# Linear attention and two feed-forward layers: how the keys are loaded, projected and multiplied out

## The chip, the core and the metric

The kernel runs on one core of one Trainium2 chip. Five engines matter: TensorE (PE, matrix products), VectorE (DVE), ScalarE (ACT), GpSimd (POOL) and SyncE (SP), whose queue issues nearly all transfers. The metric is the device time of one execution in microseconds (us); the median of three runs is compared.

## What is computed

Three stages follow one another. The attention is linear: keys and queries of 32 numbers are mapped to 64 features, the outer product of two projections of 8 numbers each.

```python
def phi(x):                                   # q, k, v: 4 batches, 4 heads, 1088 tokens, 32 numbers
    a = np.einsum('rd,bhsd->bhsr', S1, x)     # S1, S2: 8 x 32
    b = np.einsum('rd,bhsd->bhsr', S2, x)
    return np.einsum('bhsi,bhsj->bhsij', a, b).reshape(*x.shape[:-1], r * r)
q_p, k_p = (phi(q), phi(k))
kv = np.einsum('bhsf,bhsd->bhfd', k_p, v)
z = np.sum(k_p, axis=2)
num = np.einsum('bhsf,bhfd->bhsd', q_p, kv)
den = np.einsum('bhsf,bhf->bhs', q_p, z)[..., None] + 1e-06
x = num / den                                 # to 4352 tokens x 128
# feed-forward: 128 -> 1536 -> 128, gated
xn = x / sqrt(mean(x * x) + 1e-06) * rms_g
x = (silu(xn @ w_gate) * (xn @ w_val)) @ w_out
# soft mixture: 32 slots, 8 experts of 128 -> 1024 -> 128, combined back to the tokens
```

The weights and S1, S2 come as float64 words and are turned into float32 on the chip.

## The kernel before, in words

The 4352 tokens go through the feed-forward layer in nine tiles: eight of 512 tokens (two for each batch) and one of 256 with the last 64 tokens of every head (the "short" rows). A tile has 12 slots, one for each 128 of the 1536 hidden columns; a slot has three passes each for gate and value (high and low parts of float32) and three for the output, or one product in full float32 in tile 0. While these run, chains of small steps for the next tiles are set between them: `k_chain(b)` prepares the keys of a batch, `q_chain(T)` the queries of a tile.

Ahead of the first tile stands a part without feed-forward work, the front. Its order is written out by hand in the table `FRONT`, a string of tokens that `front()` reads one by one; each token calls one step, and all steps of one engine stay in this order. `kt:0`, `kt:1` and `kt:2` transpose the two halves of the keys and the short keys on DVE; `bm` places the two forms of S1 and S2 (`bdk`, `bd`) that the products take; `kp` projects the keys and `kg` the short keys on PE; `kx:0`, `kx:1` turn the projections of two heads each by a transpose on DVE (PSUM to SBUF); `ko:0`, `ko:1`, `ko:2` are the outer products of heads 0 and 1, of heads 2 and 3, and of the short keys; `kv` copies the values beside a column of ones on ACT; `ks:0`, `ks:1` sum features times values on PE; `kw`, `kb`, `kl` spread, transpose and place these sums. `qs`, `qp`, `qh`, `qo`, `qb` are the same steps for the queries of tile 0, `qa` multiplies them with the placed sums, `qd` divides, `qq` to `ql` normalize. `c:n` is one step of the conversion of weight piece n (five steps: ACT, DVE, ACT, DVE, POOL, and for gate and value pieces a split into high and low parts on ACT and POOL). `n:x` are x products of constants that keep PE busy.

Behind the front, a scheduler orders the work; it keeps each engine's queue in order, so that an instruction that waits holds all that stands behind it on its engine. The later batches (b = 1, 2, 3) go through `k_chain`.

Transfers: `load` puts each on SP. The order is S1 and S2 (on ACT's queue), keys, half of the queries, short keys, values, short values, then the weights by turns. The keys of a batch lie in a tile of 128 partitions; `c` is the half of it that one transposition and one product take. The product `project` has the 128 x 64 tile `bdk` as its stationary side and the 512 transposed columns of one half as its moving side; half c writes the output partitions 64 c to 64 c + 63 of one PSUM bank.

## Time and profile before

| what | us |
|---|---|
| runs of before, median (lowest, highest) | 314.44 (314.32, 315.17) |
| the profiled execution | 314.38 |
| its span, first to last instruction | 312.6 |
| PE busy | 302.9 |
| DVE busy | 234.8 |
| ACT busy | 178.2 |
| POOL busy | 64.5 |

Busy times are sums over the whole span, and the stages have different limits; what an engine's work is worth is read stage by stage. PE's products are pipelined, and their ends are modelled: a start of the next one is a better measure of what a product costs than its own length. In a row of a timeline, a bracket tells how long the engine stood idle before it and who released it.

### The profile page before, as it was taken

The page shows a single profiled execution, that of the slowest core. Times are in us where ns is not written, and L with a number is a line of the kernel's source. Part 1 is how long each engine was busy: PE and PEld are TensorE (multiplying, and loading weights), DVE is VectorE, ACT ScalarE, POOL GpSimd, SP SyncE. Part 2 cuts the span into 40 slices and gives each one's busy share as a digit, 9 for nine tenths or more (in the row PEclk, how much of TensorE's full clock was granted, in tenths as well). Part 3 has the DMA queues.
Part 4 walks back from the last instruction along what each step waited for, and adds up shares of the span by engine and source line. Part 5 has one row for each costly group of instructions (what it writes and reads, how often), then busy time and mean ns, then how long its engine had stood idle before and what let it go on. Part 6 is the DMA issues. An engine that isn't in the chain of part 4 may idle for free.

```text
span 312.6 us, 5481 instructions
## 1 busy us (share of the span) xinstructions
PE 302.9 (97%) x1933; PEld 235.9 (75%) x1933; DVE 234.8 (75%) x461; ACT 178.2 (57%) x399; POOL 64.5 (21%) x111
## 2 busy tenths in 40 slices
PE   8899989999999999999999999999999999999993
PEld 4676755778885778888867788888787778898482
DVE  4879956886797968878779878787787667666862
ACT  2568574385563376665533765654574655566562
POOL 3659899000601010020010100100020100003220
PEclk9999999999999999999999999999999999999999
DMA  5997100010033100010331000100991493000016
GB/s 154 243 383 220 33 1 0 2 25 11 0 125 95 26 4 0 11 25 0 118 100 25 6 0 12 25 0 14 332 221 23 134 305 101 0 2 1 2 46 242
DMA packets 43627, 23.97 MB, mean 77 GB/s; under 512 B 18896, under 2 KB 39632, under 8 KB 43600
## 3 DMA queue, kind: packets, MB, share of 16 engines
q1 hardware_dynamic: 43424, 23.56, 26.8%
q8 instruction: 15, 0.25, 0.4%
q10 hardware_dynamic: 176, 0.07, 0.1%
q14 instruction: 12, 0.10, 0.1%
HBM read 19.81 MB, written 2.23 MB: 71 GB/s over the span
## 4 chain that ended last, share of the span: by engine, by line
PE 82%; DMA 5%; SPq 4%; DVE 3%; ACT 3%; issue 2%; DVEq 0%
PE v L676 7%; PE g L676 7%; PE v L677 7%; PE o L676 7%; PE v L678 7%; PE g L677 7%; PE g L678 7%; PE o L678 7%; PE o L677 7%; SPq L78 4%; PE aux L563 4%; DMA ring<-in_moe_w_val_dram 2%; PE aux L420 2%; PE o L742 2%; PE aux L379 2%; DMA ring<-in_moe_w_out_dram 2%
## 5 line engine op out<-in xcount | busy, mean ns | idle before, releaser
L717 ACT ACTIVATE silu<-g 128x512 f32<-128x512 f32 (+1 forms) x103 | 60.9, 593 | 52.7 <-PE g L678 51.8
L718 DVE TENSOR_TENSOR hf<-v,silu 128x512 f32<-128x512 f32 (+1 forms) x91 | 61.3, 675 | 19.4 <-PE v L678 10.3
L727 ACT CAST hh<-hf 128x512 fp32r<-128x512 f32 x89 | 54.8, 616 | 36.6 <-DVE hf L718 36.3
L732 DVE TENSOR_TENSOR hl<-hf,hh 128x512 fp32r<-128x512 f32 x89 | 61.4, 691 | 15.2 <-ACT hh L727 14.4
L676 PE MATMUL g<-xh,wgh 128*128 128x512 f32 (+1 forms) x107 | 43.5, 407 | 0.9 <-ACT silu L717 0.9
L676 PE MATMUL v<-xh,wgh 128*128 128x512 f32 (+1 forms) x107 | 42.9, 401 | 0.0
L678 PE MATMUL g<-xl,wgh 128*128 128x512 f32 (+1 forms) x107 | 40.9, 382 | 0.0
L677 PE MATMUL v<-xh,wgl 128*128 128x512 f32 (+1 forms) x107 | 40.7, 381 | 0.0
L678 PE MATMUL v<-xl,wgh 128*128 128x512 f32 (+1 forms) x107 | 40.7, 380 | 0.0
L677 PE MATMUL g<-xh,wgl 128*128 128x512 f32 (+1 forms) x107 | 40.5, 379 | 0.0
L676 PE MATMUL o<-hh,woh 128*128 128x512 f32 (+1 forms) x94 | 37.1, 395 | 0.0
L678 PE MATMUL o<-hl,woh 128*128 128x512 f32 (+1 forms) x94 | 36.5, 389 | 0.0
L677 PE MATMUL o<-hh,wol 128*128 128x512 f32 (+1 forms) x94 | 35.9, 382 | 0.0
L611 POOL TENSOR_SCALAR rs<-ss 128x4 f32<-128x4 f32 (+1 forms) x8 | 2.4, 301 | 139.1 <-ACT sq L604 139.0
L676 PEld LDWEIGHTS g<-xh,wgh 128*128 128x128 f32 x107 | 20.2, 188 | 6.9 <-ACT silu L717 2.0
L676 PEld LDWEIGHTS v<-xh,wgh 128*128 128x128 f32 x107 | 20.1, 188 | 5.5 <-issue 1.9
L677 PEld LDWEIGHTS g<-xh,wgl 128*128 128x128 f32 x107 | 20.1, 188 | 4.7 <-issue 1.0
L677 PEld LDWEIGHTS v<-xh,wgl 128*128 128x128 f32 x107 | 20.1, 188 | 4.2 <-issue 1.1
L678 PEld LDWEIGHTS v<-xl,wgh 128*128 128x128 f32 x107 | 20.1, 188 | 4.1 <-issue 0.2
L678 PEld LDWEIGHTS g<-xl,wgh 128*128 128x128 f32 x107 | 20.1, 188 | 4.0 <-DVE work L318 0.2
L676 PEld LDWEIGHTS o<-hh,woh 128*128 128x128 f32 x94 | 17.7, 188 | 4.2 <-issue 1.4
L678 PEld LDWEIGHTS o<-hl,woh 128*128 128x128 f32 x94 | 17.7, 188 | 3.1 <-issue 0.2
(272 smaller groups left out, 504.1 us busy)
## 6 DMA issues: line engine op xcount, KB each, us to landing
ring<-in_moe_w_dram SPq DMA_DIRECT2D x12, 256.0 KB, 7.7
ring<-in_moe_w_dram SPq DMA_DIRECT2D x5, 512.0 KB, 5.0
ring<-in_k_dram SPq DMA_DIRECT2D x8, 256.0 KB, 3.4
ring<-in_v_dram SPq DMA_DIRECT2D x16, 128.0 KB, 2.9
ring<-in_moe_w_gate_dram SPq DMA_DIRECT2D x6, 256.0 KB, 6.7
ring<-in_moe_w_val_dram SPq DMA_DIRECT2D x6, 256.0 KB, 6.1
ring<-in_moe_w_out_dram SPq DMA_DIRECT2D x3, 512.0 KB, 7.2
qt<-in_q_dram SPq DMA_DIRECT2D x3, 512.0 KB, 5.3
```

Source lines behind the costliest of these rows:

```text
L78: i = (on or nc.sync).dma_start(out=out, in_=in_)
L379: pe.matmul(self.a["k"][64 * c : 64 * c + 64, :], bdk.rearrange("p h r -> p (h r)"), self.kT[c], start=True, stop=True)
L420: pe.matmul(self.a["kv", hp][64 * h2 : 64 * h2 + self.cols, 64 * hp : 64 * hp + 64], (va_all if t < 8 else vr_all)[:, v0 : v0 + self.cols] ...
L563: pe.matmul(o, pD[:, f, h, :], rhs, start=(f == 0), stop=(f == 1))
L676: first = pe.matmul(o, ah, bh, start=start, stop=False)
L677: pe.matmul(o, al, bh, start=False, stop=False)
L678: last = pe.matmul(o, ah, bl, start=False, stop=stop)
L717: mark["silu"] = act.activation(s[:, cs], g[:, cs], AF.Silu).ins
L718: mark["gate"] = mark["gate", T, f] = dve.tensor_tensor(out=hf32[T, f][:, cs], in0=v[:, cs], in1=s[:, cs], op=ALU.mult).ins
L727: act.copy(hh[T, f], hf32[T, f])
L732: dve.tensor_tensor(out=hl[T, f], in0=hf32.pop((T, f)), in1=hh[T, f].bitcast(F32), op=ALU.subtract)
L742: last = pe.matmul(ops[T][:, 0:w], w_c, h[:, cs], start=(c == 0), stop=(c == NF - 1))
```

## The change

Six things are changed together.

1. The keys of a batch are loaded by four transfers to 64 partitions each, where there were two to 128. Which token lies where is changed so that half c holds the tokens 512 c to 512 c + 511.
2. The short keys are loaded by one transfer to 128 partitions (256 bytes each), where there were four to 32 (two pieces of 128 bytes each). Its source has the four heads outermost, then 32 pairs of tokens.
3. The values are loaded by one transfer with 1 KB pieces, where there were four to 64 partitions with 512-byte pieces.
4. `project` issues eight products of 128 columns, where there were two of 512: for each head the two halves by turns. In the front the first two heads go to one bank and the last two to another, so that `kx:0` can begin after four of them. In the later batches the short keys' product stands ahead of them, and each product is held behind the one before it.
5. In the front the outer product of heads 2 and 3 is shared: one half on POOL, one on DVE, where POOL did both. The second part of the queries' outer product is POOL's instead of DVE's, for which ACT copies the second projection out of PSUM as well.
6. The table `FRONT` is written in another order: `kv:1` comes before `qh` and `kh`, and the weight steps `c:0` between the sums and their transposition move behind it.

```diff
--- before.py
+++ after.py
@@ -29,8 +29,8 @@
 
 
 FRONT = """
-n:17 b n:4 kz kt:0 bm kt:1 bm qs kt:2 kp kx:0 kx:1 ko:0:d ko:1:p qp kg kv:0 kh ko:2:d qh kv:1 n:4 km
-ks:0 qo:0 qo:1 qb c:0 ks:1 kw:0:a c:0 c:0 kb:0 kw:1:a n:2 kb:1 n:10 c:0 kl:0:a kl:1:d c:0 c:1 c:0 c:1 c:0
+n:17 b n:3 kz kt:0 bm kt:1 bm qs kp kt:2 kx:0 kx:1 ko:0:d ko:1:p:0 ko:1:d:1 qp kg kv:0 kv:1 qh kh ko:2:d qo:1:p n:4 km
+ks:0 qo:0:d qb c:0 ks:1 kw:0:a kb:0 kw:1:a n:2 kb:1 n:10 c:0 c:0 kl:0:a kl:1:d c:0 c:1 c:0 c:1 c:0 c:0
 qa:0 qa:1 n:26 qd:0 qd:1 qq:0:a qq:1:d qr:0 qq:2:a qq:3:d qr:1 c:1 kr:a qm:0 qm:1 qt:0 qx:0 n:2 qt:1 qx:1 c:1 c:1 ql c:2 c:2 c:2 c:1 c:2
 """
 
@@ -96,23 +96,23 @@
 
         t = ring()
         kt[b] = t.rearrange("p (h c m) -> p h c m", h=H, c=2)
+        src = k[b, :, 0:1024, :].rearrange("h (c u e n) d -> c e u h (n d)", c=2, e=2, n=4)
         for c in range(2):
-            src = k[b, :, 0:1024, :].rearrange("h (p c n) d -> c p h (n d)", c=2, n=4)[c]
-            load(out=kt[b][:, :, c], in_=src)
+            for e in range(2):
+                load(out=kt[b][64 * e : 64 * e + 64, :, c], in_=src[c, e])
 
     def load_kr(b):
-        kr[b] = sb.tile([P, 2, D], F32, tag="kr", name="kr")
-        for h in range(H):
-            load(out=kr[b][32 * h : 32 * h + 32], in_=k[b, h, 1024:, :].rearrange("(n x) d -> x n d", n=2))
+        kr[b] = sb.tile([P, 2 * D], F32, tag="kr", name="kr")
+        load(out=kr[b], in_=k[b, :, 1024:, :].rearrange("h (x n) d -> h x (n d)", n=2))
 
     def load_v(b):
 
         t = ring()
         vt[b] = t.rearrange("p (h n d) -> p h n d", h=H, d=D)
-        src = v[b, :, 0:1024, :].rearrange("h (e u c n) d -> c e u h (n d)", e=2, c=2, n=4)
-        for c in range(2):
-            for e in range(2):
-                load(out=t.rearrange("p (h e m) -> p e h m", h=H, e=2)[64 * c : 64 * c + 64, e], in_=src[c, e])
+        load(
+            out=t.rearrange("p (h n) -> p h n", h=H),
+            in_=v[b, :, 0:1024, :].rearrange("h (p j) d -> p h (j d)", j=8),
+        )
         load(out=vr[:, :, 0:D], in_=v[b, :, 1024:, :].rearrange("h p d -> p h d"))
 
     def load_q(b):
@@ -354,7 +354,7 @@
             self.kvz = kvz[b] = sb.tile([P, 2, H, 4, D1], F32, tag="kvz", name="kvz", bufs=2)
             self.pk = [work().rearrange("p (h t n) -> p h t n", h=2, t=8) for _ in range(2)]
             self.pk.append(sb.tile([P, H, 1, R * R], F32, tag="pkr", name="pkr"))
-            self.kT, self.a, self.x = {}, {}, {}
+            self.kT, self.a, self.x, self.last = {}, {}, {}, None
             self.cols = 64 if b == 0 else D1
 
         def zero(self):
@@ -366,25 +366,31 @@
                 dve.transpose(self.kT[c].rearrange("p (h m) -> p h m", h=H), kt[self.b][:, :, c])
             else:
                 self.kT[c] = sb.tile([P, 64], F32, tag="krT", name="krT")
-                dve.transpose(self.kT[c], kr[self.b].rearrange("p n d -> p (n d)"))
+                dve.transpose(self.kT[c].rearrange("p (x n) -> p n x", n=2), kr[self.b])
 
         def copy_v(self, hp, eng):
             hs = slice(2 * hp, 2 * hp + 2)
             src = vt[self.b][:, hs].rearrange("p h t d -> p (h t) d")
             eng(va[:, hs, :, 0:D].rearrange("p h t d -> p (h t) d"), src)
 
-        def project(self):
-            self.a["k"] = bank()
-            for c in range(2):
-                pe.matmul(self.a["k"][64 * c : 64 * c + 64, :], bdk.rearrange("p h r -> p (h r)"), self.kT[c], start=True, stop=True)
+        def project(self, banks=1):
+            for h in range(H):
+                if h == 0 or h == 2 and banks == 2:
+                    a = bank()
+                self.a["k", h // 2] = a
+                cs = slice(P * h, P * h + P)
+                for c in range(2) if banks == 2 else (1, 0):
+                    with tc.issue_after(self.last) if self.last else nullcontext():
+                        o = a[64 * c : 64 * c + 64, cs]
+                        self.last = pe.matmul(o, bdk.rearrange("p h r -> p (h r)"), self.kT[c][:, cs], start=True, stop=True).ins
 
         def project_r(self):
             self.a["r"] = bank()
-            pe.matmul(self.a["r"][0:64, 0:64], self.kT[2], bdf, start=True, stop=True)
+            self.last = pe.matmul(self.a["r"][0:64, 0:64], self.kT[2], bdf, start=True, stop=True).ins
 
         def turn(self, hps, dst):
             cs = slice(256 * hps.start, 256 * hps.stop)
-            dve.transpose(dst[:, cs], self.a["k"][:, cs])
+            dve.transpose(dst[:, cs], self.a["k", hps.start][:, cs])
             x = dst.rearrange("p (g r) -> p g r", r=2 * R)
             for hp in range(hps.start, hps.stop):
                 gs = slice(16 * hp, 16 * hp + 16)
@@ -393,7 +399,7 @@
         def halves_r(self):
             self.x[2] = proj_halves(self.a["r"], 4, 64)
 
-        def outer(self, g, on=dve):
+        def outer(self, g, on=dve, es=slice(0, 2)):
             x1, x2 = self.x[g]
             pp, n = x1.shape[0], x1.shape[1]
             if g < 2:
@@ -401,10 +407,8 @@
             else:
                 dst = self.pk[g][:pp].rearrange("p h j n -> p (h j) n")
 
-            m = 2 if on is pool else 1
-            for e in range(m):
-                es = slice(n // m * e, n // m * (e + 1))
-                outer(dst[:, es], x1[:, es], x2[:, es], on)
+            es = slice(n // 2 * es.start, n // 2 * es.stop)
+            outer(dst[:, es], x1[:, es], x2[:, es], on)
 
         def sum(self, hp, ts, banks=1):
 
@@ -479,14 +483,15 @@
                 pool.memset(kvT[32:64], 0.0)
             for hp in range(2):
                 k.copy_v(hp, pool.tensor_copy)
-        for c in range(2):
+        for c in (0, 1):
             yield POST, 1
             with tc.issue_after(mark["gate"]):
                 k.transpose(c)
-        k.transpose(2)
+                if c == 0:
+                    k.transpose(2)
         yield PE, 0
+        k.project_r()
         k.project()
-        k.project_r()
         yield POST, 1
         k.turn(slice(0, 2), row("x2"))
         k.halves_r()
@@ -542,9 +547,13 @@
         def halves(self):
             self.pq = work()[:, 0 : 256 * self.n].rearrange("p (f g n) -> p f g n", f=2, n=D)
             self.x1, self.x2 = proj_halves(self.a["q"], 4 * self.n, P)
-
-        def outer(self, f):
-            outer(self.pq[:, f], self.x1[:, :, 4 * f : 4 * f + 4], self.x2)
+            if self.T == 0:
+                x2 = sb.tile([P, P], F32, tag="asb", name="asb", bufs=3).rearrange("p (g r) -> p g r", r=R)
+                act.copy(x2, self.x2)
+                self.x2 = x2
+
+        def outer(self, f, on=dve):
+            outer(self.pq[:, f], self.x1[:, :, 4 * f : 4 * f + 4], self.x2, on)
 
         def back(self):
             pD = work()[:, 0 : 256 * self.n]
@@ -940,11 +949,11 @@
             "bm": lambda: next(placed, None),
             "kz": k.zero,
             "kt": lambda c: k.transpose(int(c)),
-            "kp": k.project,
+            "kp": lambda: k.project(2),
             "kg": k.project_r,
             "kx": lambda hp: k.turn(slice(int(hp), int(hp) + 1), turned),
             "kh": k.halves_r,
-            "ko": lambda g, e="d": k.outer(int(g), on[e]),
+            "ko": lambda g, e="d", half=None: k.outer(int(g), on[e], slice(int(half), int(half) + 1) if half else slice(0, 2)),
             "kv": lambda hp: k.copy_v(int(hp), act.copy),
             "ks": lambda hp: k.sum(int(hp), range(9), 2),
             "kw": lambda hp, e: k.spread_1(int(hp), copy[e]),
@@ -955,7 +964,7 @@
             "qs": q.shuffle,
             "qp": q.project,
             "qh": q.halves,
-            "qo": lambda f: q.outer(int(f)),
+            "qo": lambda f, e: q.outer(int(f), on[e]),
             "qb": q.back,
             "qa": lambda m: q.attend(int(m)),
             "qd": lambda m: q.divide(int(m)),
```

Two places show what this does to the queues. First DVE in the front, from the transposition of the first queries on (`x` are the queries, `silu` the turned projections, `work` the outer products, `pkr` that of the short keys, `kvz` the placed sums, `cvt` and `cvs` the first weight piece). Before:

```order
L535 STREAM_TRANSPOSE x_201<-x 128x512
L369 STREAM_TRANSPOSE krT<-kr 128x64
L387 STREAM_TRANSPOSE silu<-aux 128x256 x2
L318 TENSOR_TENSOR work<-silu 128x1024
L318 TENSOR_TENSOR pkr<-asb,v 64x256
L318 TENSOR_TENSOR work<-asb,g 128x512 x2
L551 STREAM_TRANSPOSE work<-work 128x1024
L220 TENSOR_SCALAR cvt<-cvt 128x512
L225 SCALAR_TENSOR_TENSOR cvs<-ring,cvt 128x512
L462 COPY kvz<-aux 32x4x33 x4
```

The same place after the change:

```order
L540 STREAM_TRANSPOSE x_196<-x 128x512
L369 STREAM_TRANSPOSE krT<-kr 128x2x32
L393 STREAM_TRANSPOSE silu<-aux 128x256
L393 STREAM_TRANSPOSE silu<-g 128x256
L318 TENSOR_TENSOR work<-silu 128x1024
L318 TENSOR_TENSOR work<-silu 128x512
L318 TENSOR_TENSOR pkr<-asb,aux 64x256
L318 TENSOR_TENSOR work<-asb 128x512
L560 STREAM_TRANSPOSE work<-work 128x1024
L220 TENSOR_SCALAR cvt<-cvt 128x512
L466 COPY kvz<-aux 32x4x33 x4
L225 SCALAR_TENSOR_TENSOR cvs<-ring,cvt 128x512
```

The two turns read two banks; half of the second outer product has come to DVE ahead of that of the short keys, and half of the queries' has gone; the weight step `cvs` has moved behind the four copies.

Second PE in the second batch of keys (b = 2 in the code), among the feed-forward products `g`, `v` and `o` of tile 2. Before:

```order
L678 MATMUL g<-xl,wgh 128x512
L379 MATMUL aux<-T,bdk 64x512
L676 MATMUL o<-hh,woh 128x512
L677 MATMUL o<-hh,wol 128x512
L678 MATMUL o<-hl,woh 128x512
L676 MATMUL o<-hh,woh 128x512
L677 MATMUL o<-hh,wol 128x512
L678 MATMUL o<-hl,woh 128x512
L383 MATMUL aux<-bd,krT 64x64
L563 MATMUL aux<-kvz,work 128x132 x4
L676 MATMUL v<-xh,wgh 128x512
L379 MATMUL aux<-T,bdk 64x512
```

And after:

```order
L687 MATMUL g<-xl,wgh 128x512
L685 MATMUL o<-hh,woh 128x512
L686 MATMUL o<-hh,wol 128x512
L389 MATMUL aux<-bd,krT 64x64
L385 MATMUL aux<-T,bdk 64x128 x8
L572 MATMUL aux<-kvz,work 128x132 x4
L687 MATMUL o<-hl,woh 128x512
L685 MATMUL v<-xh,wgh 128x512
```

Two products that stood apart have become eight in a row, behind the product of the short keys. Counted from the start, 207 feed-forward products stood ahead of the short keys' product in this batch before and 215 after; in the third batch that follows the front, 417 and 437. (An order row is one product; in float32 it is two passes in the trace.)

## Rows read from the trace of the kernel before

**Rows 1.** Busy time by stretch: stretch, its length, each engine's busy us (instructions), granted clock, DMA share, GB/s.

```profile
0.00:22.00 22.00, 18.92 (x185) 13.74 (x186) 14.28 (x41) 10.00 (x30) 10.59 (x28) 1.00 0.83 252
22.00:42.00 20.00, 19.47 (x88) 13.77 (x87) 18.16 (x33) 15.28 (x35) 18.01 (x21) 1.00 0.44 126
...
60.00:280.00 220.00, 220.00 (x1299) 177.74 (x1294) 172.04 (x313) 128.20 (x278) 17.77 (x36) 1.00 0.24 62
```

**Rows 2.** The chain of waits, PE alone: start us, us, what.

```profile
43.04 0.23 PE g L677
...
52.18 1.00 PE aux L379 x2
...
59.18 0.84 PE aux L420 x25
...
162.10 1.00 PE aux L379 x2
```

**Rows 3.** Timeline of the front, DVE and POOL: start us, us, instruction, idle before.

```profile
6.34 0.69 DVE L535 STREAM_TRANSPOSE x<-x 128x512 f32<-128x512 f32 x1
...
7.48 0.78 DVE L387 STREAM_TRANSPOSE silu<-aux 128x256 f32<-128x256 f32 x2 [0.32 <-PE aux L379]
...
8.18 1.18 DVE L318 TENSOR_TENSOR work<-silu 128x1024 f32<-128x1024 f32 x1
8.34 2.98 POOL L318 TENSOR_TENSOR work<-silu 128x512 f32<-128x512 f32 x2 [5.13 <-DVE silu L387]
```

**Rows 4.** Timeline of SP's issues at the start.

```profile
0.73 0.99 SPq L78 DMA_DIRECT2D ring<-in_k_dram  x2
1.76 0.56 SPq L78 DMA_DIRECT2D x<-in_q_dram  x1
2.37 1.91 SPq L78 DMA_DIRECT2D kr<-in_k_dram  x4
4.33 2.73 SPq L78 DMA_DIRECT2D ring<-in_v_dram  x4
...
7.76 0.60 SPq L78 DMA_DIRECT2D ring<-in_moe_w_gate_dram  x1
```

**Rows 5.** Transfers issued before 24 us: count, KB each, median us to landing.

```profile
ring<-in_v_dram SPq DMA_DIRECT2D x4, 128.0 KB, 2.9
...
x<-in_q_dram SPq DMA_DIRECT2D x1, 256.0 KB, 3.8
```

**Rows 6.** Timeline of the front, from the values to the feed-forward.

```profile
9.40 0.62 ACT L374 COPY va<-ring 128x512 f32<-128x512 f32 x1 [5.09 <-DMA ring<-in_v_dram]
...
11.42 1.15 PE L420 MATMUL g<-work,va 128*64 128x64 f32 x32
...
13.37 0.36 ACT L435 COPY kvT<-g 97x256 f32<-97x256 f32 x1
...
14.27 1.21 DVE L462 COPY kvz<-aux 32x132 f32<-32x132 f32 x4 [0.21 <-PE aux L445]
...
15.31 1.17 PE L563 MATMUL aux<-kvz,work 128*128 128x132 f32 x8
...
15.95 0.67 ACT L216 ACTIVATE cvt<-ring 128x512 f32<-128x512 f32 x1 [0.69 <-DMA ring<-in_moe_w_val_dram]
...
16.65 0.43 DVE L220 TENSOR_SCALAR cvt<-cvt 128x512 uint32<-128x512 uint32 x1 [1.18 <-ACT cvt L216]
...
17.11 0.17 DVE L578 TENSOR_SCALAR rd<-aux 128x8 f32<-128x8 f32 x1
...
17.89 0.15 DVE L578 TENSOR_SCALAR rd<-g 128x8 f32<-128x8 f32 x1
...
21.76 0.39 PE L701 MATMUL g<-xh,wgh 128*128 128x256 f32 x1
```

**Rows 7.** Timeline of PE in tile 0.

```profile
42.54 0.50 PE L676 MATMUL g<-xh,wgh 128*128 128x512 f32 x1 [0.90 <-ACT silu L717]
```

**Rows 8.** Timeline of DVE in the second batch of keys.

```profile
96.26 0.24 DVE L369 STREAM_TRANSPOSE krT<-kr 128x64 f32<-128x64 f32 x1 [2.22 <-DMA kr<-in_k_dram]
```

## The prediction

> **What bounds the kernel now.** I read the table of stretches first [rows 1]. From 60 to 280 us TensorE (PE) is busy for all 220.00 us, while VectorE (DVE) has 172.04 and ScalarE (ACT) 128.20: in this stretch a microsecond of PE work saved is a microsecond of the run saved. From 0 to 22 us no engine is full. There a chain of waits sets the time: loads, key features, their sums, the queries, until the first feed-forward product at 21.76 us [rows 6]. From 22 to 42 us GpSimd (POOL) is busy for 18.01 of 20 us and DVE for 18.16, both with the conversion of the float64 weights. PE has work nearly all the time there, too, but once it stood 0.90 us for ACT's silu, at 42.54 us [rows 7]. So the change has to be weighed at two places: the 21.76 us ahead of the feed-forward, and the PE work of three later batches.
>
> The granted clock is 1.00 in every one of these stretches [rows 1], the higher of the two levels, and the idle products that the front keeps issuing stay; I give the clock no part.
>
> **The change, part 1: key projection in the three later batches.** Before, a batch has two products of 512 columns with a 64-column stationary tile. Each is two passes and takes 1.00 us in the chain of waits; there are six such rows, of which the first and last stand in [rows 2]. Together 6.0 us. Behind one of them nothing runs beside it: the second half of the array is idle, since the two products write partitions 0 to 63 and 64 to 127 at different times. After, there are eight products of 128 columns, that is 16 passes, and neighbours write different halves.
>
> A pass of 128 columns alone is a quarter of 0.50 us, 0.125 us, so 16 in a row are 2.0 us: without overlap nothing is saved. What overlap gives is to be read from the sums of key features and values, which already alternate between the halves: 25 passes of 64 columns in 0.84 us, 33.6 ns each [rows 2], where 64 columns alone are an eighth of 0.50 us, 62.5 ns. That is 1.86 times as fast, with a new stationary tile for each pass. Applied here: 2.0 / 1.86 = 1.07 us a batch instead of 2.0, saved 0.93, in three batches **2.8 us**. The bounds: 0 if nothing overlaps, 3.0 if it is perfect.
>
> A rule speaks against taking so many small products. The Trainium skill, TensorEngine Tiling (Array Packing), Performance Considerations, says that each matmul has an overhead of about 60 cycles and that the factor should not be taken from a dimension that is already small. By it the 12 passes that are added would cost 25 ns each, 0.3 us a batch, and the 2.8 would be an estimated 1.9 us. The trace does not agree: 33.6 ns for a whole pass in [rows 2] leaves no room for 25 ns on top of the columns.
>
> Is PE kept waiting by the new order? All eight products now stand together, behind the product of the short keys, and wait for both transposes of the batch on DVE. Before, DVE's transpose of the short keys itself waited 2.22 us for its DMA, in the second batch until 96.26 us [rows 8]. But PE now comes to this place later: in the second batch 215 feed-forward products stand ahead of the short keys' product instead of 207, in the third 437 instead of 417. I take no wait.
>
> **Part 2: the front.** Step by step, in us from the start.
>
> *Issues on the sync queue (SP).* Before: keys 0.99 for two, queries 0.56, short keys 1.91 for four, values 2.73 for four; then the weights from 7.76 [rows 4]. A transfer to 64 partitions costs 2.73 / 4 = 0.68, one to 128 about 0.50. After: keys in four transfers to 64 partitions, 2.73 (+1.74); short keys in one, 0.48 (-1.43); values in one to 128 partitions, 0.50 (-2.23). Sum -1.92: the weights' issues begin at 5.84. But the queries' issue moves from 1.76 to 3.50, behind the keys.
>
> *Landings.* The queries took 3.8 us from issue to landing, behind 512 KB of keys; a values piece of 128 KB took 2.9 [rows 5]. From 3.50 that is between 6.4 and 7.3; I take 6.8. The queries' transpose on DVE started at 6.34 [rows 3], so DVE stands about 0.45 longer. The same 0.3 that DVE waited ahead of the keys' second transpose (7.48, [rows 3]) is gone, since the first bank is now complete after half the products. I take this as even: the key features' transposes at 7.55 instead of 7.48, the first outer product at 8.25 instead of 8.18.
> The values: the last piece was issued near 6.4, and ACT's copy began at 9.40, waiting for it [rows 6]. The one transfer is issued at about 4.46, 2.0 earlier, but carries 512 KB instead of 128 KB; at the 0.9 us by which 256 KB (3.8) stand above 128 KB (2.9) the 384 KB more are at most 1.3, so it lands about 8.5, 0.8 earlier.
>
> *Outer products.* POOL did both halves of the second one, 2.98 in all, 8.34 to 11.32, and the second sum waited for that at 11.42 [rows 3, 6]. Now POOL does one half (1.49, to 9.9) and DVE the other (half of 1.18, to 10.05). What is next late: the short keys' outer product, behind DVE's half and ACT's three copies, at 10.2 to 10.6; the first sum ends with it, and the second starts at 10.95 instead of 11.42. It ends 0.5 earlier. Its copy on ACT stood behind a weight step until 13.37 [rows 6] and now stands ahead of it, so the next PE step comes 1.0 earlier. On DVE the queries now have half their outer product on POOL: 10.1 to 11.6, then DVE's transpose (1.25), one weight step (0.4), the copies of the placed sums (1.21 as in [rows 6]) to 14.4, which ended at 15.48 before. So the queries' products start at 14.4 instead of 15.31, **-0.9**.
>
> *Behind them.* The first division was held until 17.11 by a weight step on DVE, which waited for ACT (16.62), which waited for a weight transfer until 15.95 [rows 6]. With weights issued 1.9 earlier I take half of it for their landing, 15.0; then that step is over by 15.9, the second division starts at 16.6 to 16.7 (two product groups of some 1.1 each behind 14.4, the first of them being the row at 15.31) instead of 17.89, and the front is **1.2 us** shorter. Bounds: 0, if the values and the weights land when they do now and DVE stands 1.0 for the queries; 2.5, if the whole 1.9 arrive and the next step is never late.
>
> *Tile 0.* POOL and DVE convert at their pace. If they start 1.2 earlier, PE's later needs are met as before, since POOL's first step of the second weight piece comes right behind the front. One conversion step on DVE is moved behind the four copies (about 1 us later), but by the times above POOL is through with what follows from it (two steps of some 1.4) by 17.7, and its next step for the front comes at about 18.1. I take the gain as kept in full and the 0.90 at 42.54 as unchanged.
>
> **The sum.** The profiled execution took 314.38 us, its span 312.6 and 1.8 around it; the median of the runs is 314.44, so no correction is needed. 314.38 - 2.8 - 1.2 = **310.4 us**.
>
> **Rivals.**
>
> *The front's gain is eaten.* For it: POOL and DVE are full from 22 to 42 us [rows 1], and PE waited already once there; the short keys and values could land no earlier, and the queries land later. Against it: the conversions of the front are moved forward with it. Time: 314.38 - 2.8 = 311.6.
> In a sentence by itself: the Trainium skill, DMA: Bandwidth & Descriptors, "Why a DMA increments its semaphore by 16 and not by 1", says that a transfer is split over the largest number of engines up to 16 that divides the slowest dimension on both sides; the short keys' new transfer reads 4 heads as its slowest dimension, so it would run on 4 engines, and the values behind it would be held there by an estimated 0.5 us, which points to this rival. No row here shows a transfer of that shape.
>
> *The halves don't overlap in these products.* Then the change does not do what it says: 16 x 0.125 = 2.0, as before. Against it: the 33.6 ns of [rows 2], in the same alternation. Time: 314.38 - 1.2 = 313.2; with the front's gain lost as well, 314.4.
>
> *PE runs into the wait for the short keys.* This ends slower. PE takes its products in order; if DVE's transpose of the short keys is late, the eight products and all feed-forward behind them stand. Price: the 2.22 that DVE stands today [rows 8], in three batches 6.7, so 314.38 - 4.0 + 6.7 = 317.1. It decides where the transfer lands later than PE's new place: in the second batch 8 more products of 0.23 [rows 2] stand ahead of it than today, so from 1.8 us of delay on at the earliest. The issue of this transfer comes after four key transfers (2.73) and the queries (0.56), 3.3 after the load begins; the last of the four issues of before began 3.1 after it [rows 4]. So it is hardly later, and I give this little.
>
> *The front gains more than I say.* The weights arrive the full 1.9 earlier, and the 0.90 at 42.54 goes, too: 314.38 - 2.8 - 1.9 - 0.9 = 308.8.
>
> **How the numbers follow.** Forecast (309.6 to 311.1) 0.60; front's gain eaten (311.1 to 312.2) 0.16; more gain (below 309.6) 0.09; no overlap, front gained (313.2) 0.07; neither (314.4) 0.04; PE waits (317.1) 0.04. The range reaches from the better case's near side, 309.0, to the end of the eaten front, 312.2; it leaves out the last three and the far end of the better case, near 0.2. A change under 0.3%, 0.94 us, can't be told from none. Faster: 0.60 + 0.16 + 0.09 and half of 0.07, 0.88. Same: the other half and 0.04, 0.08. Slower: 0.04.
>
> **What would show it.** In the three later batches the chain of waits should have about 1.07 us where it had 2.0 for the projection, with two neighbours' starts a few ns apart; 2.0 there means no overlap. The first feed-forward product should start near 20.6; the values' copy near 8.5; the queries' products near 14.4; the first division no longer behind a weight step. PE idle ahead of the short keys' product in the later batches would be the slow rival. PE idle between 21 and 43 us of more than the 0.90 would say that the conversions eat the front's gain. The forecast is wrong if the three batches save less than 2.4, or the first feed-forward product starts outside 19.5 to 21.3.

## The result, and the profile after

The changed kernel takes **311.77 us** (median; 311.68 to 312.01), the kernel before 314.40 on the same chip: 0.9914 of it, 95% interval 0.9902 to 0.9927. The profiled execution took 311.76, its span 310.0 against 312.6. That is 2.6 to 2.7 us less, inside the range of the prediction but 1.4 above its forecast of 310.4; in number it is what the first rival gave (the front's gain is eaten: 311.6).

Busy time by stretch, after; columns as in [rows 1]:

```profile
0.00:22.00 22.00, 18.62 (x195) 14.21 (x195) 15.96 (x40) 10.24 (x30) 10.70 (x28) 1.00 0.85 275
22.00:42.00 20.00, 19.57 (x89) 13.95 (x88) 18.75 (x33) 15.46 (x34) 18.18 (x22) 1.00 0.34 101
...
60.00:280.00 220.00, 219.31 (x1323) 180.41 (x1318) 171.90 (x317) 129.00 (x279) 17.93 (x36) 1.00 0.24 62
```

The clock is as before. In the first 22 us VectorE is busy for 15.96 instead of 14.28 with fewer instructions (40 against 41), although the change was to take work from it. Where the time went is read from two points, the first feed-forward product and the end. The product now starts at 21.98 instead of 21.76, so the front gained nothing; in these two profiles it **lost** 0.2. How much it lost is less sure: two other kernels below have the front of before unchanged, and their profiles have this product at 21.20 and 21.32, so single profiles of one and the same front differ by up to 0.56. From the product to the end of the span there are 288.0 us instead of 290.8.

The chain of waits, PE, second batch's key projection; answers to the rows of 1.00 in [rows 2]:

```profile
53.49 1.02 PE aux L385 x16
```

By the starts in the trace the three batches' projections take 1.02, 1.07 and 1.07 where they took 5.9 together: 2.74 less. The product of the short keys next to them, which shares their alternation, gives another 0.3. New waits of PE take 0.3 of that back:

Timeline of PE, after; the first row answers to [rows 7], the other two are new:

```profile
42.13 0.50 PE L685 MATMUL g<-xh,wgh 128*128 128x512 f32 x1 [0.55 <-ACT silu L726]
...
182.06 0.50 PE L685 MATMUL o<-hh,woh 128*128 128x512 f32 x1 [0.43 <-ACT hh L736]
...
186.31 0.50 PE L685 MATMUL g<-xh,wgh 128*128 128x512 f32 x1 [0.26 <-ACT silu L726]
```

SP's issues at the start, answering to [rows 4]:

```profile
0.73 2.75 SPq L78 DMA_DIRECT2D ring<-in_k_dram  x4
3.53 0.60 SPq L78 DMA_DIRECT2D x<-in_q_dram  x1
4.18 0.66 SPq L78 DMA_DIRECT2D kr<-in_k_dram  x1
4.89 0.43 SPq L78 DMA_DIRECT2D ring<-in_v_dram  x1
...
6.04 0.60 SPq L78 DMA_DIRECT2D ring<-in_moe_w_gate_dram  x1
```

And the front of after, one fence for each engine, answering to [rows 3] and [rows 6]. ACT and POOL:

```profile
9.86 1.14 ACT L374 COPY va<-ring 128x512 f32<-128x512 f32 x2 [5.75 <-DMA ring<-in_v_dram]
...
11.22 0.18 ACT L313 COPY asb<-aux 64x32 f32<-64x32 f32 x1
```

```profile
8.31 1.95 POOL L318 TENSOR_TENSOR work<-silu 128x512 f32<-128x512 f32 x1 [5.10 <-DVE silu L393]
11.41 1.07 POOL L318 TENSOR_TENSOR work<-asb 128x512 f32<-128x512 f32 x1 [1.15 <-ACT asb L313]
...
18.09 1.48 POOL L277 TENSOR_TENSOR wgl<-cvt,wgh 128x256 fp32r<-128x256 f32 x2
19.68 1.40 POOL L621 TENSOR_TENSOR rs<-rs,mhalf 128x2 f32<-128x2 f32 x2
```

DVE and PE:

```profile
8.15 2.66 DVE L318 TENSOR_TENSOR work<-silu 128x1024 f32<-128x1024 f32 x2
11.44 0.41 DVE L318 TENSOR_TENSOR pkr<-asb,aux 64x256 f32<-64x256 f32 x1 [0.63 <-ACT asb L313]
11.77 1.25 DVE L318 TENSOR_TENSOR work<-asb 128x512 f32<-128x512 f32 x1
13.13 1.25 DVE L560 STREAM_TRANSPOSE work<-work 128x1024 f32<-128x1024 f32 x1
...
14.60 1.20 DVE L466 COPY kvz<-aux 32x132 f32<-32x132 f32 x4
```

```profile
11.90 0.33 PE L424 MATMUL g<-pkr,vr 64*64 64x64 f32 x4 [0.22 <-DVE pkr L318]
12.17 1.15 PE L424 MATMUL v<-work,va 128*64 128x64 f32 x32
...
15.60 1.20 PE L572 MATMUL g<-kvz,work 128*128 128x132 f32 x8
...
21.98 0.39 PE L710 MATMUL g<-xh,wgh 128*128 128x256 f32 x1
```

The weights are issued from 6.04 on, 1.7 earlier, as predicted within 0.2. But the values' copy starts at 9.86 (before 9.40, forecast 8.5), the second sum at 12.17 (before 11.42, forecast 10.95), the queries' products at 15.60 (before 15.31, forecast 14.4).

How VectorE and GpSimd stand to each other shows in DVE's durations, by shape (busy us, mean ns of one):

```profile
L318 DVE TENSOR_TENSOR work<-silu 128x512 f32<-128x512 f32 x1 | 1.6, 1554 | 0.0
L318 DVE TENSOR_TENSOR work<-asb 128x512 f32<-128x512 f32 x1 | 1.2, 1250 | 0.0
...
L318 DVE TENSOR_TENSOR work<-silu 128x1024 f32<-128x1024 f32 x1 | 1.2, 1180 | 0.0
```

A product of 128x512 takes longer than one of 128x1024 beside it. The two engines do not run these products at the same time; one waits for the other. DVE's first ends at 9.33 (8.15 + 1.18); POOL's, begun at 8.31, ends at 10.26, 0.93 after that; DVE's half, begun at 9.25, ends at 10.81, 0.55 after POOL's. The later pair is the same the other way round: POOL begins first (11.41) and takes 1.07, DVE begins at 11.77 and ends at 13.02, 0.55 after POOL. Each time the later one is through 0.93 or 0.55 us after the earlier one's end, a little less than its own length (POOL's 1.07, DVE's 0.67 below). This is also where the 2.98 of [rows 3] came from. POOL in the kernel before, one instruction at a time, then DVE's products of the queries there:

```profile
8.34 1.95 POOL L318 TENSOR_TENSOR work<-silu 128x512 f32<-128x512 f32 x1 [5.13 <-DVE silu L387]
10.25 1.07 POOL L318 TENSOR_TENSOR work<-silu 128x512 f32<-128x512 f32 x1
```

```profile
10.47 1.27 DVE L318 TENSOR_TENSOR work<-asb,g 128x512 f32<-128x512 f32 x2
```

The 2.98 was 1.95 behind DVE and 1.07 without DVE in its way, and no two halves of 1.49. DVE's two products there read one input from PSUM (`g`); they took 0.67 each, and the first of them ran wholly beside POOL's second half.

The Trainium skill states it so (SBUF — State Buffer, Who interferes with whom): a VectorE instruction with two SBUF inputs contends with a GpSimd instruction that reads SBUF, over a shared port pair that is locked for one of them, and the order of issue decides who waits. The trace agrees, with the numbers above.

### The profile page after: what moved, and what is told of

It is laid out like the page before. It is cut to its first block, busy times and chain, and to the rows that moved or that the text cites. A ratio compares the mean times of both kernels' runs of the same rounds, so it can differ in the third digit from the quotient of the medians.

```text
span 310.0 us, 5557 instructions
## 1 busy us (share of the span) xinstructions
PE 299.7 (97%) x1980; PEld 237.6 (77%) x1980; DVE 236.2 (76%) x461; ACT 178.6 (58%) x400; POOL 64.7 (21%) x111
## 4 chain that ended last, share of the span: by engine, by line
PE 71%; DVE 10%; ACT 6%; POOL 5%; DMA 3%; issue 3%; SPq 1%; DVEq 0%; ACTq 0%; POOLq 0%
PE g L685 6%; PE v L685 6%; PE v L686 6%; PE g L686 6%; PE o L685 6%; PE g L687 6%; PE v L687 6%; PE o L686 6%; PE o L687 6%; PE aux L572 3%; PE o L751 2%; PE aux L424 2%; POOL wgl L277 2%; DMA ring<-in_v_dram 2%; PE fo L1270 1%
## 5 line engine op out<-in xcount | busy, mean ns | idle before, releaser
L685 PE MATMUL v<-xh,wgh 128*128 128x512 f32 (+1 forms) x107 | 42.0, 392 | 0.1
L686 PE MATMUL g<-xh,wgl 128*128 128x512 f32 (+1 forms) x107 | 41.5, 387 | 0.0
L685 PEld LDWEIGHTS o<-hh,woh 128*128 128x128 f32 x94 | 17.7, 188 | 4.3 <-ACT hh L736 0.9
L687 PEld LDWEIGHTS o<-hl,woh 128*128 128x128 f32 x94 | 17.7, 188 | 3.4 <-issue 0.2
```

The lines of the kernel that those rows point to most:

```text
L685: first = pe.matmul(o, ah, bh, start=start, stop=False)
L686: pe.matmul(o, al, bh, start=False, stop=False)
L687: last = pe.matmul(o, ah, bl, start=False, stop=stop)
```

## The experiments

The kernels ran in three groups, each group on one chip with the kernel before (314.50, 314.35 and 314.89 there): first the keys' part, whole products, half by half and pairs outermost; then the two corners of the square, the short keys on ACT's queue and the neighbours in the kernel before; last the rest. Within a group medians are compared directly, across groups by the ratio to before.

**The keys' part alone.** Front and loads as before; in the three later batches eight products, with the short keys' product ahead of them and the short keys' transposition between those of the two halves, as in the change:

```diff
-            for c in range(2):
-                pe.matmul(self.a["k"][64 * c : 64 * c + 64, :], bdk..., self.kT[c], ...)
+            for h in range(H):
+                for c in (1, 0):
+                    self.last = pe.matmul(o, bdk..., self.kT[c][:, cs], ...).ins
```

> The kernel before, with only the three later batches' projection changed to eight products by turns (and the short keys' product ahead of them); loads, front and table stay. Theory A (all of the gain of 2.6 us comes from these products, the front gives nothing): the chain of each batch has about 1.03 us instead of 2.0 for them, 314.4 - 2.9 = 311.5 us (311.1 to 311.9). Theory B (the products give less, and part of the gain is the front's): 312.3 or more.

Measured: 311.18 (311.11 to 311.47), ratio 0.9897 (0.987 to 0.992), three projections of 1.02. From its first weight product, the first product of the feed-forward (21.20), to the end there are 288.1 us, as in the change (288.0). The keys' part is the whole gain, and the rest of the change nets nothing or a little loss.

**Is it the 128 columns?** The changed kernel with two whole products next to each other in the later batches:

```diff
+            if banks == 1:
+                for c in (1, 0):
+                    o = a[64 * c : 64 * c + 64, :]
+                    self.last = pe.matmul(o, bdk..., self.kT[c], ...).ins
+                return
```

> The changed kernel, but the later batches again project by two products of 512 columns, now next to each other. If products overlap only where narrow ones alternate, a batch takes 2.0 us as before: 311.8 + 2.9 = 314.7. If neighbours in different halves overlap whatever their width, the second pass of one runs beside the first of the other, three passes of 0.43 = 1.3 us a batch: 311.8 + 0.8 = 312.6.

Measured: 310.58 (310.34 to 310.69), ratio 0.9875 (0.985 to 0.990). Neither expectation: faster than the change. The timeline of PE:

```profile
53.50 1.08 PE L382 MATMUL aux<-T,bdk 128*64 128x512 f32 x4
```

Four passes of 512 columns in 1.08, start to next start 1.01: in this batch they overlap in pairs, whose starts are 7 ns apart, without being cut. What was missing before was not small products but neighbours: one product stood 2 to 4 us away from the other, with feed-forward products between.

**The order of the halves.** All eight products of one half, then those of the other:

```diff
+            pairs = [(h, c) for h in range(H) for c in range(2)] if banks == 2 else [(h, c) for c in (1, 0) for h in range(H)]
```

> The changed kernel, but in the later batches the eight products of 128 columns are issued half by half: four for one half of the array, then four for the other. If alternation is what overlaps them, only the two at the seam run together: 15 passes of 0.107 to 0.11, 1.65 us a batch instead of 1.03, 311.8 + 1.9 = 313.7. If narrow products overlap in any order: 311.8.

Measured: 311.43 (311.29 to 311.78), ratio 0.9902 (0.987 to 0.993).

```profile
53.55 1.58 PE L386 MATMUL aux<-T,bdk 128*64 128x128 f32 x16
```

1.45 to 1.51 a batch, between 1.02 and the some 1.75 that 16 passes would take one behind the other at the 0.109 between two starts of one half here: order decides, but not as sharply as expected. The second half's first pass starts at 54.05, together with the fifth of eight of the first. The time is below both expectations. The 0.7 us of waits at 182 and 186 are absent here, which is less than the 1.25 by which the three projections are longer than in the change; where the rest comes from is open.

**Before, with its two products made neighbours** in the later batches, behind the product of the short keys (whose transposition moves as above), and nothing else:

```diff
+            for c in (1, 0):
+                o = self.a["k"][64 * c : 64 * c + 64, :]
+                self.last = pe.matmul(o, bdk..., self.kT[c], ...).ins
```

> The kernel before with one edit: in batches 1 to 3 the two whole 512-column products stand right behind the short keys' product with nothing between them; no product is cut, and front and loads are as before. Theory A (products to different array halves overlap when they stand next to each other, whatever their width): about 1.01 to 1.06 us per batch instead of 1.9 to 2.0, first weight product at 21.2 to 21.8, time 310.0 to 311.5. Theory B (128 columns are needed, or the whole products' gain came with the rest of the change): 1.9 to 2.0 us per batch and 313.9 to 314.6.

Measured: 312.62 (312.41 to 313.09), ratio 0.9947 (0.993 to 0.996): a miss for both. The projection takes 1.01 in every batch, as theory A had it, but in the last PE runs into the slow rival of the prediction. PE, then DVE:

```profile
52.74 1.08 PE L385 MATMUL aux<-T,bdk 128*64 128x512 f32 x4
...
157.18 0.30 PE L389 MATMUL aux<-bd,krT 128*64 128x64 f32 x2 [1.36 <-DVE krT L369]
```

```profile
156.79 0.24 DVE L369 STREAM_TRANSPOSE krT<-kr 128x64 f32<-128x64 f32 x1 [2.67 <-DMA kr<-in_k_dram]
```

DVE waits 2.67 for the short keys' four transfers and PE 1.36 for DVE. In the changed kernel, with one transfer, DVE's waits for it are 0.3 in all, and PE has none. The keys' part alone has the four transfers as well, DVE waits 1.81 and 2.08 for them, and PE still has none; the kernel with the old loads below has 0.32. In all ten kernels here with one transfer PE never waits. So the one transfer seems to be worth something in the later batches, and not always; it was not tried by itself.

**The front: loads against steps.** Two kernels that, with the change and the keys' part alone, make a square. First the changed kernel with the loads of before:

```diff
-            for e in range(2):
-                load(out=kt[b][64 * e : 64 * e + 64, :, c], in_=src[c, e])
+            load(out=kt[b][:, :, c], in_=src)
...
-        load(out=kr[b], in_=k[b, :, 1024:, :].rearrange("h (x n) d -> h x (n d)", n=2))
+        for h in range(H):
+            load(out=kr[b][32 * h : 32 * h + 32], ...)
```

> The changed kernel with the loads of keys, short keys and values (and the short keys' transposition) as before; its steps of the front, its shared outer products and its eight products per batch stay. With the run whose front steps and loads are all as before (keys only: first weight product at 21.20 us) and the next run here it splits the front's change in two. Theory A: the loads brought something (keys transposed earlier) and the steps of the front lost it again; then old loads under the new steps are the worst of the four, first weight product at 22.2 to 22.8 us and a time of 312.2 to 312.8. Theory B: the loads lost it (values' copy at 9.86 us instead of 9.40) and the steps are neutral; then the values' copy starts at 9.4 or earlier, the first weight product at 21.2 to 21.5 and the time is 311.0 to 311.3.

Measured: 312.23 (311.69 to 314.15), ratio 0.9947 (0.992 to 0.998), the time of theory A; the profiled execution took 313.57, with the first weight product at 22.93. And the new loads under the old steps:

```diff
-n:17 b n:3 kz kt:0 bm kt:1 bm qs kp kt:2 kx:0 kx:1 ko:0:d ko:1:p:0 ko:1:d:1 qp kg kv:0 kv:1 qh kh ko:2:d qo:1:p n:4 km
+n:17 b n:4 kz kt:0 bm kt:1 bm qs kt:2 kp kx:0 kx:1 ko:0:d ko:1:p qp kg kv:0 kh ko:2:d qh kv:1 n:4 km
```

> The new loads under the steps of the front as before (two 512-column key products in batch 0, queries' outer product on VectorE alone, short keys and values' copies in the old order on ScalarE); eight products in batches 1 to 3. Theory A (the loads bring something, the steps lose it): keys transposed near 7.6 us instead of 8.2, first weight product at 20.5 to 20.9 us, time 310.4 to 310.9. Theory B (the loads lose it through the later values): values' copy at 9.8 us and first weight product at 21.5 to 22.0, time 311.5 to 312.0.

Measured: 310.93 (310.79 to 311.46), ratio 0.9894 (0.988 to 0.991), first weight product at 21.20, between the two theories. The square by ratio: old loads and old steps 0.9897, new loads and old steps 0.9894, both new 0.9914, old loads and new steps 0.9947. The new steps come out worse under either load (0.0020 and 0.0050 of 314, 0.6 and 1.6 us), but in both pairs the intervals overlap, so that the direction is likely and the size is not shown; the loads gain nothing under the old steps. Part of the worst corner is arrival of data, which a single profile can't tell from the steps; ACT there:

```profile
17.05 0.68 ACT L216 ACTIVATE cvt<-ring 128x512 f32<-128x512 f32 x1 [1.88 <-DMA ring<-in_moe_w_val_dram]
```

That transfer is used at 15.95 before [rows 6], 15.19 and 15.37 in the two other kernels with the old loads, 17.05 here. With the new loads it landed at 13.7 to 14.0 in the change and the three kernels of the first group that have them. So the term "weights land earlier" held, but what waits for it then waits for something else.

**Sharing alone.** New loads, old steps, and only the keys' outer product shared:

```diff
-... ko:0:d ko:1:p qp kg ...
+... ko:0:d ko:1:p:0 ko:1:d:1 qp kg ...
```

> The new loads under the front's steps as before, with one edit: GpSimd's part of the keys' outer product (two halves of 1.51 us each) is shared, one half for GpSimd and one for VectorE. Theory A (the two slow each other down and the short keys' and the queries' steps on VectorE move back by what it takes on): GpSimd's half takes 1.9 to 2.0 us, VectorE's 1.2 to 1.6, both done 0.6 us earlier than GpSimd alone, but the first weight product stays within 0.2 us of 21.2 and the time at 310.8 to 311.3. Theory B (the sums start as much earlier as the outer product is done): first weight product at 20.5 to 20.8, time 310.3 to 310.6.

Measured: 311.79 (311.40 to 312.04), ratio 0.9913 (0.989 to 0.994), as theory A said of the engines, but worse than either theory said of the time; first weight product at 22.27. Without sharing (the kernel above), DVE, POOL, PE:

```profile
8.36 1.18 DVE L318 TENSOR_TENSOR work<-silu 128x1024 f32<-128x1024 f32 x1
10.35 0.41 DVE L318 TENSOR_TENSOR pkr<-asb,v 64x256 f32<-64x256 f32 x1 [0.80 <-ACT asb L313]
```

```profile
8.52 2.98 POOL L318 TENSOR_TENSOR work<-silu 128x512 f32<-128x512 f32 x2 [5.32 <-DVE silu L395]
```

```profile
11.63 1.15 PE L428 MATMUL g<-work,va 128*64 128x64 f32 x32
```

With sharing, the same engines:

```profile
8.84 2.66 DVE L318 TENSOR_TENSOR work<-silu 128x1024 f32<-128x1024 f32 x2
11.42 0.40 DVE L318 TENSOR_TENSOR pkr<-asb,v 64x256 f32<-64x256 f32 x1
```

```profile
9.00 1.95 POOL L318 TENSOR_TENSOR work<-silu 128x512 f32<-128x512 f32 x1 [5.79 <-DVE silu L395]
```

```profile
11.88 0.33 PE L426 MATMUL aux<-pkr,vr 64*64 64x64 f32 x4 [0.46 <-DVE pkr L318]
12.14 1.15 PE L426 MATMUL g<-work,va 128*64 128x64 f32 x32
```

Measured from DVE's first product, the second outer product is done after 2.66 (11.50 - 8.84) instead of 3.14 (11.50 - 8.36), 0.5 gained; the short keys' product starts after 2.58 instead of 1.99, 0.6 lost, and everything of DVE's behind it with that. The second sum needs both: it starts 3.30 after instead of 3.27. The first weight product comes 13.43 after instead of 12.84, 0.6 lost. The 0.48 by which DVE's first product is later in this profile stood there before the sharing (short keys' landing). The ratios of the two kernels differ by 0.0019, 0.6 us, but their intervals overlap; so the mechanism is shown by the trace, its price only roughly by the times.

**What else in the steps?** The short keys' copies on ACT before, not behind, the second of the values:

```diff
-... kv:0 kv:1 qh kh ko:2:d qo:1:p n:4 km
+... kv:0 kh ko:2:d qh kv:1 qo:1:p n:4 km
```

> The changed kernel with one edit in the order of the front's steps: the copies of the short keys' halves on ScalarE stand again between the two copies of the values and not behind both. Theory A (this order is most of what the new steps lose): the short keys' outer product starts at 10.3 to 10.9 us instead of 11.44, the queries' products with the keys' sums (instruction out of kvz) at 15.1 to 15.3 instead of 15.60, the first weight product at 21.4 to 21.7 instead of 21.98, time 311.2 to 311.5. Theory B (GpSimd's later steps hold the front): the first weight product within 0.2 us of 21.98, time 311.6 to 311.9.

Measured: 311.53 (311.39 to 311.80), ratio 0.9907 (0.988 to 0.993); short keys' product at 10.82, queries' products at 15.29, first weight product at 21.63, all as theory A had them, the time just above its upper end. The gain stops at the next pair on the shared port. POOL, DVE:

```profile
10.85 1.90 POOL L318 TENSOR_TENSOR work<-asb 128x512 f32<-128x512 f32 x1 [0.50 <-ACT asb L552]
```

```profile
11.15 0.67 DVE L318 TENSOR_TENSOR work<-asb 128x512 f32<-128x512 f32 x1
12.79 1.25 DVE L560 STREAM_TRANSPOSE work<-work 128x1024 f32<-128x1024 f32 x1 [0.96 <-POOL work L318]
```

Now DVE's half takes 0.67 and POOL's 1.90; DVE's transpose waits 0.96 for it. By the recorded starts POOL is the earlier one, by 0.30, and still the one that waits; in the change it was earlier by 0.36 and did not wait. So which of a pair goes first can't be told from recorded starts that are so close.

One edit more, the second weight block's steps put back ahead of the placing:

```diff
-... kw:0:a kb:0 kw:1:a n:2 kb:1 n:10 c:0 c:0 kl:0:a ...
+... kw:0:a c:0 c:0 kb:0 kw:1:a n:2 kb:1 n:10 c:0 kl:0:a ...
```

> The kernel of the run above with one more edit: the second weight block's steps (its two sums and two low parts on GpSimd) stand again ahead of the placing of the sums and not behind it. Theory A: GpSimd is through with them at 17.6 to 18.2 us instead of 19.57, the power step waits for VectorE alone and starts at 18.9 to 19.2 us instead of 19.68, first weight product at 21.2 to 21.5, time 310.9 to 311.2, the same as with all of the front's steps as before. Theory B (GpSimd had no part in it): as the run above.

Measured: 312.33 (311.63 to 313.48), ratio 0.9931 (0.991 to 0.996), first weight product at 21.81: theory A falls. GpSimd was through at 18.14 as it said, but DVE's weight step now stood ahead of the four copies of the sums, which began at 14.74 instead of 14.26, and the power step came at 19.51. Either place costs one of the two engines.

**The values' landing.** Short keys with 32 pairs of tokens outermost instead of 4 heads:

```diff
-k[b, :, 1024:, :].rearrange("h (x n) d -> h x (n d)", n=2)
+k[b, :, 1024:, :].rearrange("h (x n) d -> x h (n d)", n=2)
```

> The changed kernel, but the one transfer of the short keys reads its source with the 32 pairs of tokens outermost and the four heads inside, so that both sides have a slowest dimension that 16 divides; the same bytes, the same piece size (the short keys land on other partitions, so that their part of the sums is not the reference's; the work is the same). Theory A (the shape with four heads outermost spreads over few engines and holds the values behind it): the values' copy starts at 9.1 to 9.4 instead of 9.86, the first feed-forward product 0.3 to 0.6 earlier than 21.98, 311.2 to 311.5 us. Theory B (the values are late by their own size and issue): 9.8 to 9.9, 311.8.

Measured: 312.24 (311.33 to 314.91), ratio 0.9932 (0.991 to 0.996).

```profile
9.44 1.14 ACT L374 COPY va<-ring 128x512 f32<-128x512 f32 x2 [5.36 <-DMA ring<-in_v_dram]
```

```profile
182.66 0.50 PE L685 MATMUL o<-hh,woh 128*128 128x512 f32 x1 [1.03 <-ACT hh L736]
```

The values come 0.42 earlier and the first feed-forward product at 21.55, 0.43 earlier, as theory A said; but the wait at 182, 0.43 in the change, is 1.03 here, and the time is no better. The 0.42 can be followed from step to step, since DVE's first product starts at 8.15 in both. DVE's product of the short keys:

```profile
11.02 0.41 DVE L318 TENSOR_TENSOR pkr<-asb,aux 64x256 f32<-64x256 f32 x1 [0.20 <-ACT asb L313]
```

It starts 0.42 earlier (11.44 in the change), the second sum 0.42 (11.75), the queries' products 0.41 (15.19). So in the change it is the values that hold the front, by way of ACT, which copies them ahead of the short keys' halves. The traces also keep the updates of each transfer's semaphore: for the short keys one at 5.24 and four from 6.86 to 7.07 in the change, sixteen from 6.47 to 6.89 here. Of the values' sixteen the last three came at 9.70 to 9.79 in the change, the others by 9.15; here the last comes at 9.36. That is theory A in all but the time.

And the short keys issued first of all on ACT's queue (at 1.70), so that the values' issue begins at 4.18 instead of 4.89:

```diff
-            load(out=kr[b], in_=...)
+            load(out=kr[b], in_=..., on=act if b == 0 else None)
...
+    load_kr(0)
     load_k(0)
     rest_q = load_q(0)
-    load_kr(0)
```

> The changed kernel with one edit: batch 0's short keys are issued on ScalarE's queue instead of SyncE's, so that the values' transfer is issued some 0.6 us earlier. Theory A: the values' copy decides the front: it starts at 9.0 to 9.4 us, the first weight product 0.4 to 0.7 us earlier (21.3 to 21.6), time 311.1 to 311.4. Theory B: the front is held by the outer products shared between VectorE and GpSimd and by GpSimd's later steps: the values' copy is earlier, the first weight product within 0.2 us of 21.98, time 311.6 to 312.0.

Measured: 311.94 (311.47 to 312.37), ratio 0.9927 (0.991 to 0.995): theory B by its numbers. The values' copy starts at 9.01, 0.85 earlier, and the first feed-forward product at 21.81. But the edit also moved something else. DVE's transposition of the second half of the keys:

```profile
6.46 0.71 DVE L366 STREAM_TRANSPOSE T<-ring 128x512 f32<-128x512 f32 x1 [0.83 <-DMA ring<-in_k_dram]
```

It started at 5.83 in the change. With it DVE's first product comes 0.58 later (8.73), and its short keys' product (11.31) stands right behind the contended pair. So this run does not show that the values are of no account; it shows that 0.85 there is worth little once the pair comes later.

**The best of the parts.** New loads and old steps, as in the second corner of the square, with one more edit:

```diff
-            for h in range(H):
-                for c in (1, 0):
-                    self.last = pe.matmul(o, bdk..., self.kT[c][:, cs], ...).ins
+            for c in (1, 0):
+                self.last = pe.matmul(self.a["k"][64 * c : 64 * c + 64, :], bdk..., self.kT[c], ...).ins
```

> The new loads under the front's steps as before, and in batches 1 to 3 two whole 512-column key products next to each other instead of eight of 128 columns. If the parts add up: first weight product at 21.2 us, 286.8 us from there to the end (as the run with whole products had it), 1.76 us beside them: 309.8 us. If whole products win nothing here (the gain of that run came from its order of steps): 310.8 to 311.0.

Measured: **310.11** (309.95 to 310.22), ratio 0.9860 (0.983 to 0.989), the fastest of all.

```profile
53.02 1.08 PE L385 MATMUL aux<-T,bdk 128*64 128x512 f32 x4
```

From the first weight product (21.59) to the end 286.75, as expected; the front came 0.4 later than expected. The waits at 182 and 186 are absent here, as with whole products above.

## Why the prediction was right and wrong

The time fell into the range because the range reached to the end of a front that gains nothing. The gain of the keys was foreseen with its mechanism, that of the front was not there, and by the prediction's own sign (first feed-forward product outside 19.5 to 21.3) its forecast failed. The first rival had the number, 311.6, and one of its reasons, that the values could land no earlier. Its other reason, that the conversions from 22 to 42 us eat the gain, did not come up: there was no gain to eat.

**Key projection: right in size and in mechanism.** 2.8 was forecast, 2.74 measured, and 0.3 came on top from the short keys' product. The pairs of starts are 7 ns apart or less, as foreseen. What the prediction did not ask is whether the products must be cut for it: two uncut products do the same if they are neighbours. The 60 cycles that the Trainium skill gives each matmul (TensorEngine Tiling (Array Packing), Instruction Overhead) would have cost an estimated 0.3 us a batch for twelve more passes, if they came on top of each; between 16 passes and 4 the runs show 0.01 to 0.02 us (1.024 against 1.009). So the trace does not show them on top of passes of 128 columns; passes of under 64 columns were not tried. A pass alone was taken at 0.125 us; in half-by-half order its starts are 0.109 apart.

**The front: wrong.** 1.2 was forecast, -0.2 measured (-0.8 against the keys' part alone, at 21.20). Three steps failed. At the short keys' product, which the second sum waits for, the first two meet: it was to start at 10.2 to 10.6 and came at 11.44.

- *The values' landing.* Forecast 8.5, measured 9.86, of which 0.4 is a later issue (4.89 for 4.46). The main slip is in the working: 0.9 us was read for 128 KB more, and the 384 KB more were then put at 1.3, where three times 0.9 are 2.7. With 2.7 the same working gives 10.1. In the change DVE's outer products are done at 10.81, and DVE then stands 0.63 for ACT, which is busy with the values' two copies and three others from 9.86 on. Values 0.42 earlier (32 pairs outermost) made the front 0.43 shorter, and the short keys' copies moved ahead of the second copy of the values made it 0.35 shorter. The rule that the prediction set apart (the Trainium skill, DMA: Bandwidth & Descriptors, Why a DMA increments its semaphore by 16 and not by 1) pointed the right way: four late updates against sixteen agree with it. Its estimated 0.5 was given without a working; the run shows 0.42.
- *Outer products.* "POOL does one half (1.49, to 9.9) and DVE the other (half of 1.18, to 10.05)" took a mean of two unlike durations (1.95 and 1.07) and let the engines run side by side. They run in turn: done at 10.26 and 10.81. The second sum's operands came 0.5 earlier, DVE's next step could start 0.7 later than the 10.1 that was taken. Under the old steps, where ACT is not in the way, this alone moved the first weight product back by 0.6. The queries' half on POOL needed ACT's copy of its second input into SBUF; by that DVE's own half got two SBUF inputs and joined the conflict (1.25 instead of 0.67).
- *The copy of the sums and the division.* The first division no longer waits for weights, as said. It starts at 16.89, 0.2 earlier than before, and the chain behind it ends up behind GpSimd: the weight steps that were moved behind the copies end at 19.57, and the power step starts at 19.68 (before 19.46). The prediction had POOL through by 17.7 because it had the copies done by 14.4; they end at 15.80.

What each of these cost in time is not settled by the medians, whose intervals overlap; the order of events is read from the traces.

**Tile 0: not shown either way.** The 0.90 at 42.54 became 0.55. But it is 0.24 and 0.23 in the two kernels that keep the loads and steps of before (keys' part alone, neighbours), so it moves from profile to profile without the front's change. The two waits at 182 and 186 were not foreseen. They are there in all kernels with the new loads and eight products in alternation, absent with whole products and in half-by-half order, and the first of them is 1.03 in one. What makes it can be read from ACT, in the change and then with whole products:

```profile
179.84 1.52 ACT L458 COPY kvz<-aux 32x264 f32<-32x264 f32 x4
181.38 0.62 ACT L736 CAST hh<-hf 128x512 fp32r<-128x512 f32 x1
```

```profile
179.95 0.62 ACT L743 CAST hh<-hf 128x512 fp32r<-128x512 f32 x1 [0.87 <-DVE hf L734]
```

In the change ACT's four copies of the placed sums stand ahead of the cast that the product at 182.06 waits for; with whole products the cast comes first and the copies behind it (180.48). All seven kernels with that wait have the first order; the two with whole products under the new loads and the one in half-by-half order have the second. Why the scheduler sets them so was not tried.

**The slow rival.** It did not show in the change, but the kernel before with neighbouring products had it, at 1.36 in one batch, and the one with the old loads at 0.32: the price of 2.22 a batch was too high and the 4% not foolish.

## What to carry to other kernels

Two products that use different halves of the array cost one if they stand next to each other in PE's order; look for a partner before cutting products small. Before work is shared between VectorE and GpSimd, look where the inputs are: two SBUF inputs on VectorE beside a GpSimd instruction that reads SBUF run in turn, and the sharing then mostly fills the engine that had less slack. Before a step's copies are put in a new order, ask which of them waits for data: what stands behind it on that engine waits, too. Never take half of a group's time for one of its instructions where the group ran partly beside another engine.

## What the runs showed of the hardware that was not expected

- VectorE and GpSimd products with all inputs in SBUF take turns by whole instructions: 1.95 against 1.07 for GpSimd, 1.25 and 1.55 against 0.67 for VectorE. A VectorE product with one input in PSUM is not touched (0.67 beside GpSimd in the kernel before). In the change a small VectorE step (128x2, 19.12) took 0.48 instead of 0.17 and ended at 19.60, just behind GpSimd's weight step (19.57); it reads as the same wait, but was not tried.
- In half-by-half order the second half's first pass starts with the fifth of eight passes of the first half: 1.45 to 1.51 us a batch. It reads as if passes for the free half may start ahead of a few that wait for the other; how many was not tried.
- A transfer whose landing nobody had moved came anywhere between 15.1 and 17.0 us in four kernels with the same loads, three of them with the same front (first feed-forward product at 21.20, 21.32 and 21.76); a single profile of a front that waits for data has to be read with that in mind.
- A transfer of 32 KB in 256-byte pieces whose source has four heads outermost ended with four late updates of its semaphore (6.86 to 7.07), with 32 pairs outermost with sixteen (6.47 to 6.89), and the 512 KB behind it were used 0.42 earlier.
